# A chunked-attention and gated-MLP kernel: its first steps rebuilt, with signs of weights on GpSimd, loads for two units at a time, all attention products on quarters of the array, and a written order for every engine

## The chip, the cores and the metric

One core of a Trainium2 chip. The metric is the device time of one launch in microseconds (us), median of a few runs. A profiled execution gives the trace that is read here; its own time stands beside its span below.

## The reference

Attention within chunks of 64 tokens, then a gated MLP on the result (4608 tokens, model width 512, hidden width 1536):

```
scores = scale * np.matmul(q_c, k_c.transpose(0, 1, 2, 4, 3))   # 8 batches, 8 heads, 9 chunks of 64, D = 64
scores = scores - np.max(scores, axis=-1, keepdims=True)
attn = np.exp(scores)
attn = attn / (np.sum(attn, axis=-1, keepdims=True) + 1e-09)
out = np.matmul(attn, v_c)
...
gate = 1.0 / (1.0 + np.exp(-(x @ w_gate)))
val = x @ w_val
return (gate * val @ w_out).astype(np.float32)
```

## The kernel before

**Number formats.** Weights arrive as 64-bit floats, as pairs of 32-bit words. The kernel makes of each a high part in fp32r and a low part (value minus high part), and does the same with activations; a product is then three matmuls: high by high, high by low, low by high.

**Tiling.** The tokens are cut into 9 blocks of 512. A block has four *units* (half of its tokens, half of the heads: `units`, L142). For a unit the kernel makes the scores (`products`, L171), a softmax (`scores` L236, `softmax` L257), transposes of the weights of attention (`transposes`, L270), and the values (`values`, L283), which write the block's activations `xt` as high and low part. Units 0 to 7 make the blocks 0 and 1. In these, two heads share one product: the keys of a unit lie in `kbd`, a tile whose off-diagonal halves were set to zero (L76 to L82), and likewise `pbd` for the transposed weights of attention. From unit 8 on, units go in pairs through `products2` (L186) and `values2` (L205), in which each product uses a 64 x 64 quarter of the array and nothing is zero-filled.

**The MLP.** The hidden width is cut into 12 pieces f. `up` (L312) is 12 matmuls over the tokens of a step (G for the gate, V for the value); `hidden` (L326) makes both and the product behind them: sigmoid on ACT (L329), product on DVE (L331), high part on ACT (L334), low part on DVE (L335). `down` (L340) adds the step to the output, three matmuls per 128 tokens. For block 0 the pieces f = 0 and 1 go in two *half steps* of 256 tokens each (`a`, `b`), and all later f in steps of 512 tokens. Blocks 0 to 2 are done in this way; blocks 3 to 8 go in pairs by another scheme (from L505 on), which the change leaves alone.

**Weights.** A piece f has three parts: gate (0), value (1), out (2), each a load of 128 x 1024 words (512 KB, `load_weights` L101). `convert_weights` (L112) turns a part into high and low: two scalings on ACT (L131, L132), a shift on DVE (L133), the sign bit put in (L134), an addition (L136), the high part on ACT (L138) and the low part on DVE (L139). Raw words lie in the tiles of later pieces (slots of f = 9 to 11), so a load must wait until the part that was there is converted.

**What sets the order.** `START` (L29) and `MIDDLE` (L35) are lists of steps: L loads q and k of a unit, V its v, S or s makes the scores (s with the exponentials on ACT and their sums), E, t/T and A the rest; W loads weights, C converts a part, H0.3 is f = 3 of block 0, D a down product. Inside START no engine's order is written: the tool that builds the program orders the instructions of all engines by its own costs, with the list as priority. From MIDDLE on, TensorE follows the list exactly, and from `rest` on DVE and ACT do too. While START runs, weights of block 0 are also stored again in DRAM for the later blocks (`given`, `stream`, L378).

At the very start eight products of a zero tile into an unused bank (`sink`, L92) are queued on TensorE.

Of the kernel before, what the change touches and what calls it, by code (L numbers as in the profile page):

```python
# [15 lines left out]
P = 128  # L16
# [11 lines left out]

START = """  # L29
L0 L1 V0 W0o S0 s1 V1 E0 W0u t0 C0.0 E1 L2 t1 L3 C0.1 A0 W1u S2 C0.2 s3 A1 C1.0 H0.0a E2 W1o E3 C1.1  # L30
T2 W2u T3 D V3 L4 V2 C2.0 A2 C1.2 A3 L5 H0.1a H0.0b W3o D W3u C2.1 C3.0 H0.1b D s4 W4u W2o H0.2 C3.2
C2.2 W4o C3.1 C4.0 D W5u E4 C4.1 C5.0 C5.1 H0.3 D s5 C4.2 t4 E5 W6u H0.4 D W7u C6.0 V5 W6o C7.0 C6.1
H0.5 D W5o L6 C5.2 L7 C6.2 H0.6 V4 W8u C7.1 D W7o C8.0 t5 C8.1 C7.2 H0.7 D W9u
"""
MIDDLE = """  # L35
C9.0 W8o C8.2 W9o C9.1 W10u A4 A5 H0.8 W10o D C10.0 C9.2 C10.2 W11u H0.9 C10.1 D H0.10 C11.0 C11.1 D
W11o H0.11 S7 V7 S6 D L9 E6 H1.0a C11.2 D V6 E7 T6 T7 D H1.1a A6 A7 D H1.0b L8 V8 H1.1b V9 D
"""

VECTOR_TRANSPOSES = 8  # L40
# [10 lines left out]
def chunk_attn_moe(ctx: ExitStack, tc: tile.TileContext, q, k, v, w, out, outt):  # L51
# [17 lines left out]
    early = xp.tile([P, 4, 8, D], F32, tag="x", name="early")  # L69
    zeros = early[:, 0, 0].bitcast(mybir.dt.bfloat16)  # L70
    nc.vector.memset(zeros, 0.0)

    kp = ctx.enter_context(tc.tile_pool(name="kp", bufs=1))
    kbd = [kp.tile([P, 2, 2, 256], F32, tag=f"k{i}", name=f"kbd{i}") for i in range(2)]
    pbd = [kp.tile([P, 8, 2, D], F32, tag=f"p{i}", name=f"pbd{i}") for i in range(2)]
    for i in range(2):  # L76
        eng = nc.gpsimd if i else nc.vector
        eng.memset(kbd[i][0:D, :, 1, :], 0.0)
        eng.memset(kbd[i][D:P, :, 0, :], 0.0)
    for i in range(2):  # L80
        nc.gpsimd.memset(pbd[i][0:D, :, 1, :], 0.0)
        nc.gpsimd.memset(pbd[i][D:P, :, 0, :], 0.0)  # L82
    make_identity(nc, ident)
# [17 lines left out]
    def load_weights(f, kind):  # L101
        if kind == "o":
            raws[f, 2] = stage("spare" if f == NF - 1 else f"o{NF - 1 if f == NF - 2 else NF - 1 - f % 2}", 1024)
        elif f == NF - 1:
            raws[f, 0], raws[f, 1] = stage(f"o{f}", 1024), stage("spare", 1024)
        else:
            raw = stage(f"u{NF - 1 if f == NF - 2 else NF - 1 - f % 2}", 2048)
            raws[f, 0], raws[f, 1] = raw[:, :1024], raw[:, 1024:]
        for part in (2,) if kind == "o" else (0, 1):
            nc.sync.dma_start(raws[f, part], w[f, :, part * 1024:(part + 1) * 1024])  # L110

    def convert_weights(f, part):  # L112

        words = raws.pop((f, part)).rearrange("p (n two) -> p two n", two=2)
        low, high = words[:, 0, :], words[:, 1, :]
        if part == 0:
            both = wp.tile([P, 2, 1024], F32R, tag=f"u{f}", name="w")
            wt[f, 0], wt[f, 1] = both[:, :, :512], both[:, :, 512:]
        elif part == 2:
            wt[f, 2] = wp.tile([P, 2, 512], F32R, tag=f"o{f}", name="w")  # L120
        hi, lo = wt[f, part][:, 0], wt[f, part][:, 1]
        if f < 9:
            slot = 9 if f == 8 else 9 - f % 2
            if part == 0:
                spare[f] = stage(f"u{slot}", 2048)
            val = stage(f"o{slot}", 1024)[:, :512] if part == 2 else spare[f][:, 512 * part:512 * (part + 1)]
        else:
            val = mp.tile([P, 512], U32, tag="ob", name="w_val")
# [831 lines left out]
```

## Time and profile before

| | |
|---|---|
| median of 3 runs | 913.32 us (912.51 to 915.12) |
| the profiled execution | 913.89 us, span 912.1 us |
| TensorE busy | 885.3 us |
| VectorE (DVE) busy | 622.0 us |
| ScalarE (ACT) busy | 417.1 us |
| GpSimd (POOL) busy | 273.6 us |
| mean granted TensorE clock | 0.989 |

PE is TensorE, PEld its weight loads, which run beside its matmuls. In a row of the timeline stand start, duration, engine, line, operation, tiles (out <- in), shapes, count, and in brackets how long the engine was idle before and what ended it. In a row of groups stand count, busy time, mean ns of one, and idle time with its releasers. In a row of windows stand the stretch, its length, busy time (instructions) of each engine named, the granted clock (1.00 is full), the busy share of the DMA engines and GB/s. A busy TensorE isn't TensorE at its peak: matmuls overlap. fp32 products leave two records each, so that 16 products of scores show as 32.

### The profile page before, as it was taken

What the parts mean: (1) busy time and instruction counts of PE and PEld (TensorE: products, weight loads), DVE (VectorE), ACT (ScalarE), POOL (GpSimd) and SP (SyncE); (2) the same over time, 40 slices, a digit from 0 to 9 for tenths busy, and PEclk for the clock granted to TensorE, in tenths of its full rate; (3) what the DMA queues carried; (4) which work ended last, traced back from release to release, by engine and by line L of the source; (5) the groups of instructions that cost most, each with busy time, mean ns of one, the idle gap of its engine ahead of it and who ended that gap; (6) DMA issues with size and microseconds to landing.
All of it is one profiled execution on the core that took longest, in us unless ns stands there. A gap on an engine that the chain in (4) does not pass through costs nothing. (4 is left out here: it accounts for less than half of the span.)

```text
span 912.1 us, 15127 instructions
## 1 busy us (share of the span) xinstructions
PE 885.3 (97%) x5748; PEld 724.9 (79%) x5748; DVE 622.0 (68%) x906; ACT 417.1 (46%) x738; POOL 273.6 (30%) x343
## 2 busy tenths in 40 slices
PE   6999999999999999999999999999999999999998
PEld 3788779888778787877778888888788888888886
DVE  5899885368758787666657995566579943434884
ACT  5889754345425463344453632455335321112441
POOL 1000000168757892256561000353510002432000
PEclk6899999999999999999999999999999999999999
DMA  8599895145554466578784568765545685454553
GB/s 257 204 286 301 279 333 187 47 140 175 173 182 140 145 200 213 182 247 271 226 309 144 202 221 276 257 242 204 178 139 207 210 295 205 171 206 161 185 208 116
DMA packets 93432, 189.74 MB, mean 208 GB/s; under 512 B 8240, under 2 KB 48688, under 8 KB 89520
## 3 DMA queue, kind: packets, MB, share of 16 engines
q1 hardware_dynamic: 93360, 188.78, 61.5%
q8 instruction: 46, 0.75, 0.3%
q14 instruction: 26, 0.21, 0.1%
HBM read 146.28 MB, written 42.47 MB: 207 GB/s over the span
## 5 line engine op out<-in xcount | busy, mean ns | idle before, releaser
L320 PE MATMUL g<-xt,w 128*128 128x512 f32 (+1 forms) x960 | 209.9, 373 | 7.0 <-ACT hf L329 5.1
L320 PEld LDWEIGHTS g<-xt,w 128*128 128x128 f32 x960 | 168.0, 190 | 43.6 <-ACT hf L329 8.9
L651 PE MATMUL d<-hd,wd 128*128 128x512 f32 x756 | 172.4, 389 | 0.1
L651 PEld LDWEIGHTS d<-hd,wd 128*128 128x128 f32 x756 | 141.7, 188 | 30.3 <-DVE hd L631 0.9
L505 PE MATMUL cy<-xc,wr 128*128 128x512 f32 x648 | 159.4, 389 | 0.6 <-DVE s1u L523 0.6
L505 PEld LDWEIGHTS cy<-xc,wr 128*128 128x128 f32 x648 | 121.5, 188 | 26.2 <-DVE s1u L523 1.0
L505 PE MATMUL cx<-xc,wr 128*128 128x512 f32 x432 | 110.7, 391 | 0.0
L505 PE MATMUL cz<-xc,wr 128*128 128x512 f32 x432 | 109.9, 390 | 0.2
L346 PE MATMUL acc<-w,hx 128*128 128x512 f32 x432 | 106.0, 393 | 0.0
L533 POOL TENSOR_TENSOR hid<-u,hid 128x512 f32<-128x512 f32 x15 | 19.4, 1290 | 269.5 <-DVE u L562 269.5
L505 PEld LDWEIGHTS cz<-xc,wr 128*128 128x128 f32 x432 | 80.9, 188 | 17.8 <-issue 1.0
L505 PEld LDWEIGHTS cx<-xc,wr 128*128 128x128 f32 x432 | 80.5, 188 | 17.0
L346 PEld LDWEIGHTS acc<-w,hx 128*128 128x128 f32 x432 | 80.0, 188 | 16.9 <-ACT xt L308 0.2
L415 POOL TENSOR_TENSOR a_val<-a_val 128x128 f32<-128x128 f32 x36 | 18.7, 520 | 239.1 <-DVE a_val L406 180.6
L521 ACT COPY s1u<-cx 128x512 f32<-128x512 f32 x36 | 21.1, 587 | 112.3 <-PE cx L505 107.9
L630 ACT CAST hd<-hid 128x1024 fp32r<-128x1024 f32 x48 | 49.9, 1051 | 49.2 <-PE d L651 37.3
L631 DVE TENSOR_TENSOR hd<-hid,hd 128x1024 fp32r<-128x1024 f32 x48 | 58.4, 1221 | 12.4 <-ACT hd L630 12.2
L778 ACT COPY pt<-pr 32x256 f32<-32x256 f32 x130 | 52.4, 403 | 26.0 <-DVE pr L766 24.2
L331 DVE TENSOR_TENSOR hf<-g,hf 128x512 f32<-128x512 f32 (+1 forms) x40 | 25.3, 632 | 41.7 <-PE g L320 26.4
L523 DVE TENSOR_TENSOR s1u<-cy,s1u 128x512 f32<-128x512 f32 x36 | 24.7, 686 | 38.2 <-PE cy L505 38.2
L334 ACT CAST hx<-hf 128x512 fp32r<-128x512 f32 (+1 forms) x40 | 23.2, 580 | 60.1 <-DVE hf L331 60.1
L562 DVE TENSOR_TENSOR hid<-cz,u 128x512 f32<-128x512 f32 x18 | 12.4, 692 | 55.3 <-PE cz L505 55.2
(125 smaller groups left out, 1188.4 us busy)
## 6 DMA issues: line engine op xcount, KB each, us to landing
wr<-sums SPq DMA_DIRECT2D x72, 512.0 KB, 4.6
wd<-stream SPq DMA_DIRECT2D x30, 1024.0 KB, 4.8
w_raw<-w_in SPq DMA_DIRECT2D x36, 512.0 KB, 5.1
wr<-given SPq DMA_DIRECT2D x36, 512.0 KB, 3.7
qt<-q_in SPq DMA_DIRECT2D x36, 256.0 KB, 4.0
vt<-v_in SPq DMA_DIRECT2D x36, 256.0 KB, 3.4
given<-w SPq DMA_DIRECT2D x36, 256.0 KB, 4.8
wr<-given SPq DMA_DIRECT2D x36, 256.0 KB, 2.8
```

The lines of the kernel that those rows point to most:

```text
L320: nc.tensor.matmul(ps[:, tok], lhsT=wt[f, which][:, wpart, c:c + P], rhs=x[:, part, i, tok], start=n == 0, stop=n == 11)
L331: nc.vector.tensor_tensor(out=hf, in0=pv, in1=hf, op=ALU.mult)
L334: nc.scalar.copy(hh[:, tok], hf)
L346: nc.tensor.matmul(acc[m, t], lhsT=hx[:, ts], rhs=wt[f, 2][:, wpart], start=f == 0 and i == 0, stop=f == NF - 1 and i == 2,)
L505: nc.tensor.matmul(bank, lhsT=lhs(wpart, c), rhs=x[:, part, c], start=start and k == 0, stop=stop and k == 5, skip_group_check=True)
L521: nc.scalar.copy(s1, x)
L523: nc.vector.tensor_tensor(out=u2, in0=y, in1=s1, op=ALU.add)
L533: eng.tensor_tensor(out=h, in0=value, in1=h, op=ALU.mult)
L630: nc.scalar.copy(t[:, 0], at)
L631: nc.vector.tensor_tensor(out=t[:, 1], in0=at, in1=t[:, 0].bitcast(F32), op=ALU.subtract)
L651: nc.tensor.matmul(bank, lhsT=w[:, o:o + P], rhs=x[:, part], start=p == 0 and opening and i == 0, stop=p == 5 and i == 2, skip_group_check ...
L778: eng(pb[dst, :, c, i, :], ps[src, h::2, k, :])
```

## The change

A new list, `OPENING`, takes the place of the first two fifths of START, and **every engine's order** in it is written: TensorE, DVE, ACT, GpSimd and the queue of loads follow it as it stands. The rest of START comes behind it on DVE and ACT. Its words are single steps: `w.f.part` loads a part; `qk.p` and `vv.p` load q and k, and v, of pair p (units 2p and 2p+1); `a p b d h l` are the steps of a conversion; `scores max sub exp sum inv mul turn ca cd av` are the attention of a pair, where i = 0 and i = 1 are the two heads that share a product's place (i = 0 has one exponential over 128 x 512, i = 1 eight with sums); `xh` and `xl` write the high and low part of an activation; `G g V m hh hl D` are a half step; `fill.n` are n products of no use into the bank `sink`, now read from the identity tile.

```diff
+OPENING = """
+w.0.0 qk.0 w.0.1 vv.0 qk.1 w.0.2 w.1.0 w.1.1 w.1.2 a.0.0 p.0.0 b.0.0 d.0.0 fill.14 scores.0 h.0.0 max.0.1 a.0.1
...
+"""
 START = """
-L0 L1 V0 W0o S0 s1 V1 E0 W0u t0 C0.0 E1 L2 t1 L3 C0.1 A0 W1u S2 C0.2 s3 A1 C1.0 H0.0a E2 W1o E3 C1.1
...
+L4 W3o p4 W4u H0.2 C3.1 C3.2
```

**A conversion.** The shift and the sign step become one DVE instruction; GpSimd makes the sign, by multiplying the high word by 0.0 in place. All 36 conversions change so.

```diff
-        nc.vector.tensor_scalar(out=val, in0=val, scalar1=3, scalar2=None, op0=ALU.logical_shift_left)
-        nc.vector.scalar_tensor_tensor(
-            out=val, in0=high, scalar=0x80000000, in1=val, op0=ALU.bitwise_and, op1=ALU.bitwise_or)
-        nc.vector.tensor_tensor(out=val, in0=val, in1=low, op=ALU.add)
+        if step == "p":
+            nc.gpsimd.tensor_scalar(
+                out=high.bitcast(F32), in0=high.bitcast(F32), scalar1=0.0, scalar2=None, op0=ALU.mult)
+        elif step == "b":
+            nc.vector.scalar_tensor_tensor(
+                out=val, in0=val, scalar=3, in1=high, op0=ALU.logical_shift_left, op1=ALU.bitwise_or)
+        elif step == "d":
+            nc.vector.tensor_tensor(out=val, in0=val, in1=low, op=ALU.add)
```

**Loads.** q, k and v of a pair are one load each of 512 KB (the host lays them out so), in one buffer instead of two. q and k of pair 0, and the first weights, now stand ahead of all else in the queue, in the order w.0.0, q, k, w.0.1, v, q, k, w.0.2, w.1.0, w.1.1, w.1.2; before, it was q and k of units 0 and 1 in six loads, then v and weights in turn.

```diff
-        qt = ap2.tile([P, 2, 256], F32, name="qt")
-        nc.sync.dma_start(qt, q[g, u].rearrange("p (a n) -> p a n", a=2))
-        if j < 8:
-            kb = kbd[j % 2]
-            for i in range(2):
-                s = slice(i * D, (i + 1) * D)
-                nc.sync.dma_start(kb[s, :, i, :], k[g, u, s].rearrange("p (a n) -> p a n", a=2))
...
+        g = j // 2
+        qt = ap2.tile([P, 2, 2, 256], F32, tag="pr" if g == 1 else "qt", name="qt", bufs=1)
+        nc.sync.dma_start(qt, q[g].rearrange("p u (a n) -> p u a n", a=2))
+        keys[g] = kp.tile([P, 2, 2, 256], F32, tag="k1" if g else "k0", name="kt")
+        nc.sync.dma_start(keys[g], k[g].rearrange("p u (a n) -> p u a n", a=2))
```

**Quarters.** `products`, `values`, `kbd` and `pbd` are gone, with their zero fills; units 0 to 7 go in pairs through `products2` and the products of `values2` too. The eight products at the start become `fill`:

```diff
-    for _ in range(8):
-        nc.tensor.matmul(sink, lhsT=zeros, rhs=zeros.unsqueeze(1).broadcast_to([P, 4, P]), start=True, stop=True)
+    def fill(times):
+        for _ in range(times):
+            nc.tensor.matmul(
+                sink, lhsT=blank[:, :P], rhs=blank[:, P:].unsqueeze(1).broadcast_to([P, 4, P]), start=True, stop=True)
...
+    with tc.manual_schedule(engines={mybir.EngineType.PE}):
+        with tc.manual_schedule(engines={
+                mybir.EngineType.DVE, mybir.EngineType.Activation, mybir.EngineType.Pool, mybir.EngineType.SP}):
+            for token in OPENING.split():
+                begin(token)
```

**The order on TensorE**, from the first scores on, before (`sc` scores, `tp` transposes, `av` values, `g_296` and `g_311` the gate and value banks of the first half step, `acc` down products):

```order
L179 MATMUL sc<-kbd_90,qt 64x128 x8
L179 MATMUL sc<-kbd_91,qt 64x128 x8
L274 MATMUL tp<-ident,early 128x128 x8
L290 MATMUL av<-pbd_92,vt 64x128 x8
L179 MATMUL sc<-kbd_90,qt 64x128 x8
L320 MATMUL g_296<-xt,w 128x256
L320 MATMUL g_311<-xt,w 128x256
L179 MATMUL sc<-kbd_91,qt 64x128 x8
L320 MATMUL g_296<-xt,w 128x256 x5
L320 MATMUL g_311<-xt,w 128x256 x3
L290 MATMUL av<-pbd_93,vt 64x128 x8
```

and now, with fills (14, 12, 4 and 6 of them) where lines are left out at first:

```order
L190 MATMUL sc<-kt,qt 64x64 x32
...
L298 MATMUL tp<-ident,early 128x128 x8
L205 MATMUL av<-pt,vt 64x64 x32
...
L394 MATMUL g_360<-xt,w 128x256 x12
L394 MATMUL g_377<-xt,w 128x256 x12
L298 MATMUL tp<-ident,early 128x128 x8
L205 MATMUL av<-pt,vt 64x64 x32
L420 MATMUL acc<-w,hx 128x512 x6
L394 MATMUL g_482<-xt,w 128x256 x12
```

Before, units came one by one and the first half step was cut up between scores and values; now the scores of both pairs stand first, the first half step is whole and lies between the values of pair 0 and the transposes of pair 1, and from the values of pair 1 on TensorE has only half steps and down products until the scores of units 4 and 5, which stand ahead of H0.2.

**The order on DVE**, from the first maximum on, before (`mx` maxima, `early` the softmax, `sums` and `inv` its sums and their reciprocals, `w_raw` and `w` weights):

```order
L240 TENSOR_REDUCE mx<-sc 128x8
L249 TENSOR_TENSOR early<-sc,mx 128x512
L240 TENSOR_REDUCE mx<-sc 128x8
L251 TENSOR_SCALAR mx<-mx 128x8
L262 TENSOR_REDUCE sums<-early 128x8
L265 TENSOR_SCALAR sums<-sums 128x8
L267 RECIPROCAL inv<-sums 128x8
L268 TENSOR_TENSOR early<-early,inv 128x512
```

and now, from its first weight on:

```order
L142 SCALAR_TENSOR_TENSOR w_raw<-w_raw 128x512
L145 ISA w_raw<-w_raw 128x1024
L270 TENSOR_REDUCE mx<-sc 128x8 x2
L275 TENSOR_SCALAR mx<-mx 128x8
L272 TENSOR_TENSOR early<-sc,mx 128x8x64
L149 TENSOR_TENSOR w<-w_raw,w 128x512
L142 SCALAR_TENSOR_TENSOR w_raw<-w_raw 128x512
L145 ISA w_raw<-w_raw 128x1024
L287 TENSOR_SCALAR sums_177<-sums_177 128x8
L289 RECIPROCAL inv<-sums_177 128x8
L285 TENSOR_REDUCE sums_177<-early 128x8
L291 TENSOR_TENSOR early<-early,inv 128x8x64
```

Weights come ahead of the first maximum and between the steps of the softmax (L142 is step b, L145 d, L149 l); before, the first conversion stood behind the softmax of units 0 and 1.

**The order on ACT**, before, around its first sigmoid (`hf` the gate, `xt` activations):

```order
L260 ACTIVATE early<-early 128x512
L138 CAST w<-w_raw 128x512
L308 CAST xt<-av 128x2x256
L254 ACTIVATE early,sums<-sc,mx 128x64 x8
L329 ACT_TABLE_LOAD
L329 ACTIVATE hf<-g_296 128x256
L138 CAST w<-w_raw 128x512
```

and now, from the same exponential on (`pt` the transposed weights of attention, `hx` the hidden step):

```order
L277 ACTIVATE early<-early 128x8x64
L314 CAST xt<-av 128x256 x4
L281 ACTIVATE early,sums_253<-sc,mx 128x64 x8
L133 ACTIVATE w_raw<-w_raw 128x512
L134 ACTIVATE w_raw<-w_raw 128x512
L328 ACT_TABLE_LOAD
L328 ACTIVATE hf<-g_360 128x256
L147 CAST w<-w_raw 128x512
L303 COPY pt<-tp 128x256
L336 CAST hx<-hf 128x256
L303 COPY pt<-tp 128x256
```

The second pair's exponentials, two scalings and the table load now stand ahead of the copies of the transposes that the values of pair 1 read.

More of the change, by code (lines that the diff above doesn't have):

```diff
@@ L67, in chunk_attn_moe @@
     ident = const.tile([P, P], F32, name="ident")
[L69 to L71 removed]
+    early = xp.tile([P, 2, 2, 8, D], F32, tag="x", name="early")
+    make_identity(nc, ident)
+    blank = ident.bitcast(mybir.dt.bfloat16)
     kp = ctx.enter_context(tc.tile_pool(name="kp", bufs=1))
[L74 to L83 removed]
     warm = sm.tile([P, 1], F32, name="warm", bufs=1)
@@ L142, in chunk_attn_moe @@
+    def convert_weights(f, part):
+        for step in "apbdhl":
+            converting(f, part, step)
     units = [(m, h, u) for m in range(NB) for h in range(2) for u in range(2)]
@@ L188, in products2 @@
             sc = [ps_g.tile([P, 512], F32, tag="g1", name="sc", bufs=1), ps_o.tile([P, 512], F32, tag="acc", name="sc")]
+        elif j == 2:
+            sc = [ps_o.tile([P, 512], F32, tag="acc", name="sc") for _ in range(2)]
         else:
@@ new lines, in begin @@
+    def begin(token):
+        word, *at = token.split(".")
+        if word == "fill":
+            fill(int(at[0]))
+        elif word == "qk":
+            load(2 * int(at[0]))
+        elif word == "vv":
+            load_values(2 * int(at[0]))
+        elif word == "w":
+            load_part(int(at[0]), int(at[1]))
+        elif word in tuple("apbdhl"):
+            converting(int(at[0]), int(at[1]), word)
+        elif word in ("G", "V", "g", "m", "hh", "hl", "D"):
+            half(word, int(at[0]), at[1])
+        else:
+            opening(word, *map(int, at))
@@ L833, in run @@
             load_values(int(arg))
-        elif what in "Ss":
-            scores(int(arg), what == "s")
+        elif what in "Pp":
+            scores2(int(arg), (0, 1) if what == "p" else ())
         elif what == "E":
@@ L839, in run @@
             transposes(int(arg), what == "t")
-        elif what == "A":
-            values(int(arg))
+        elif what == "B":
+            values2(int(arg))
         elif what == "W":
@@ L851, in run @@
             finish()
-    for op in START.split():
-        run(op)
     kept = [(p, which, c) for p in range(6) for which in range(2) for c in range(2)]
@@ L924, in chunk_attn_moe @@
     with tc.manual_schedule(engines={mybir.EngineType.PE}):
+        with tc.manual_schedule(engines={
+                mybir.EngineType.DVE, mybir.EngineType.Activation, mybir.EngineType.Pool, mybir.EngineType.SP}):
+            for token in OPENING.split():
+                begin(token)
+        with ExitStack() as behind_opening:
+            for kind in (mybir.EngineType.DVE, mybir.EngineType.Activation):
+                behind_opening.enter_context(tc.issue_after(
+                    next(x for x in reversed(nc.cur_bb.bb.instructions) if x.engine == kind)))
+            for op in START.split():
+                run(op)
         for op in MIDDLE.split():
```

292 lines of the change are left out of this document (175 added, 117 removed).

## The prediction

> **What bounds the kernel now.** I read the page first, then the busy time of each engine in four stretches, cut where the first product over all 512 tokens starts (51.42 us), where the twelve f of the first block are through (140.38), and at 190. Columns: stretch, length, busy us (instructions) of PE, PEld, DVE, ACT and POOL, then the granted TensorE clock, the share of the DMA engines, GB/s.
>
> ```profile
> 0.00:51.42 51.42, 40.16 (x296) 32.04 (x297) 36.36 (x74) 34.51 (x86) 3.82 (x12) 0.80 0.74 235
> 51.42:140.38 88.96, 87.43 (x430) 70.22 (x429) 79.81 (x147) 70.49 (x142) 0.00 (x0) 1.00 0.94 304
> 140.38:190.00 49.62, 49.62 (x408) 42.86 (x407) 22.79 (x43) 15.56 (x25) 7.01 (x10) 1.00 0.33 112
> 190.00:912.10 722.10, 708.06 (x4618) 579.77 (x4616) 483.06 (x645) 296.58 (x486) 262.76 (x321) 1.00 0.59 201
> ```
>
> TensorE bounds everything from 51 us on (87.43 of 88.96, then 49.62 of 49.62). In the first stretch it is idle for 11.3 us and runs at a mean clock of 0.80. The change rebuilds that stretch; whatever TensorE reaches earlier at 51.42 is carried to the end of the 912.1 us, unless a later stage cannot follow. Next, the clock there, in single microseconds (length, PE busy, clock, DMA share, GB/s), and the first two blocks of q.k products:
>
> ```profile
> 1.00:2.00 1.00, 1.00 (x3) 1.00 0.34 45
> 2.00:3.00 1.00, 1.00 (x4) 1.00 0.83 266
> 7.00:8.00 1.00, 0.00 (x0) 0.67 0.99 372
> 8.00:9.00 1.00, 0.39 (x4) 0.50 0.98 387
> 27.00:28.00 1.00, 1.00 (x14) 0.59 0.91 248
> ```
>
> ```profile
> 5.58 1.10 PE L179 MATMUL sc<-kbd,qt 128*64 128x128 f32 x16 [1.26 <-DMA kbd<-k_in]
> 8.62 1.97 PE L179 MATMUL sc<-kbd,qt 128*64 128x128 f32 x16 [1.94 <-DMA kbd<-k_in]
> ```
>
> The clock falls to half at about 7.3 us, in the gap between two short bursts, and comes back only at about 27.8: the same 16 records take 1.10 us before and 1.97 after. The waits of TensorE in the first 50 us say what the bursts wait for:
>
> ```profile
> PE tp L274 <- DVE early L268: 5.2, 3, 2.9
> PE sc L179 <- DMA kbd<-k_in: 3.2, 2, 1.9
> ...
> PE g L320 <- ACT w L138: 0.8, 1, 0.8
> PE g L320 <- ACT xt L308: 0.7, 2, 0.4
> ```
>
> So the opening is a chain through DMA, softmax on DVE and ACT, and weight conversion, with TensorE at half clock meanwhile. The point that I follow is the first product over 512 tokens (H0.2), since TensorE has the same work ahead of it in both kernels: six units of scores, four of transposes and values, four half steps, three down products.
>
> **The change part by part.** Prices of that work at full clock:
>
> ```profile
> 47.16 3.04 PE L320 MATMUL g<-xt,w 128*128 128x256 f32 x24
> 50.03 1.56 PE L346 MATMUL acc<-w,hx 128*128 128x512 f32 x6
> 51.42 0.40 PE L320 MATMUL g<-xt,w 128*128 128x512 f32 x1
> ```
>
> ```profile
> 135.63 1.97 PE L179 MATMUL sc<-kbd,qt 128*64 128x128 f32 x32
> ...
> 146.00 1.03 PE L274 MATMUL tp<-ident,pr 128*128 128x128 f32 x8
> ...
> 151.21 1.97 PE L290 MATMUL av<-pbd,vt 128*64 128x128 f32 x32
> ```
>
> ```profile
> 211.14 1.16 PE L199 MATMUL sc<-kt,qt 64*64 64x64 f32 x64
> ...
> 223.34 1.16 PE L214 MATMUL av<-pt,vt 64*64 64x64 f32 x64
> ```
>
> From start to start a half step (G and V) takes 2.87 us and a down product 1.39. A pair of units costs 1.97 in the old form and 1.16 on quarters, scores and values alike.
>
> *Quarters, after H0.2:* scores of units 6 and 7, values of 4 and 5 and of 6 and 7: three blocks, each 0.81 less on an engine that is never idle there: **-2.4 us**.
>
> *Loads:* the stream runs from about 2.0 us, and at 387 GB/s in the ninth microsecond, when weights are moved. I give every load of 0.524 MB 1.34 us, and 0.4 until its reader starts (an estimate). The new order is w, q, k, w, v, q, k: k of pair 0 is there at 6.4, the second weights at 7.8, k of pair 1 at 11.8. The old transfers moved only 45 and 266 GB/s in the second and third microsecond; if the start is as slow again, all this comes 1.5 later.
>
> *The chain in the new order.* Durations on ACT and DVE (count, busy us, mean ns of one, idle before):
>
> ```profile
> L132 ACT ACTIVATE w_raw<-w_raw 128x512 uint32<-128x512 uint32 x36 | 24.4, 681 | 0.7 <-DMA w_raw<-w_in 0.7
> ...
> L329 ACT ACT_TABLE_LOAD x5 | 6.4, 1283 | 0.7 <-PE g L320 0.6
> ...
> L334 ACT CAST hx<-hf 128x256 fp32r<-128x256 f32 x8 | 3.3, 410 | 7.2 <-DVE hf L331 7.2
> ```
>
> ```profile
> L139 DVE TENSOR_TENSOR w<-w_raw,w 128x512 fp32r<-128x512 f32 x27 | 18.3, 687 | 5.7 <-ACT w L138 5.3
> ```
>
> and eight exponentials with their sums, on ACT in one block:
>
> ```profile
> 11.60:14.20 2.60, 2.47 (x16) 0.50 1.08 322
> ```
>
> Scores of pair 0 run from 6.4 to 7.6. DVE then has nine instructions of 0.69 in its list up to mul.0.0 and five on 8 columns, which I put at 0.2: 6.2 + 1.0, so 14.8. ACT isn't last: a.0.1 from 7.8 to 9.2, exponentials to 11.7, one of 128x512 to 12.4. Transposes 1.03, last copy 0.4, values 1.16: av.0 ends at 17.6. ACT goes on with four high parts (1.6, to 19.3), eight exponentials (21.8), a.1.1 (1.4, 23.2), the table (24.4), then g, h.0.2, two copies and hh (2.3, 26.7). TensorE meanwhile does G and V of 0.a and the transposes, which fit, and av.1 starts at 26.8. From there it has a dense queue: av.1 1.1, three half steps 8.6, three down products 4.2, scores of units 4 and 5 1.1, together 15.0: H0.2 at 41.8. For hand-overs I add 1.5, what the two waits on w and xt above cost the old order: **43.3** against 51.42, **-8.1 us**. If instructions overlap on ACT as back-to-back ones do, and nothing waits, it is 41, or -10.4.
>
> *Fill products:* 36 instead of 8, in front of work that isn't there yet. Over 512 columns I price one at 0.24, twice one of the 24 in a half step (2.87 / 24 = 0.12). The twelve behind the first scores then end at 7.6 + 2.9 = 10.5, before k of pair 1 at 11.8, and the four behind the second before mul.0.0, so the loads and DVE hide them and I count nothing. At half clock that cover is gone: twelve take 5.8, and what follows comes about 2 us later.
>
> *Signs by GpSimd:* the shift and the sign step become one on DVE. The old shift alone, in the middle stretch:
>
> ```profile
> 51.42:140.38 88.96, 10.86 (x27) 1.00 0.94 304
> ```
>
> So 0.40 for each of the 36 conversions leaves DVE, and a GpSimd instruction over 128x512 comes between ACT's first scaling and DVE's or-step. The trace has no such instruction; its nearest rows are a cast there, and a DVE subtract of two SBUF tensors and a DVE product with one operand in PSUM, in the stage in which GpSimd works too (min/median/max ns):
>
> ```profile
> L419 POOL CAST a_high<-a_val x30: 609/616/1604, 180.8 to 345.7; 128x512 fp32r<-128x512 f32 x30
> ```
>
> ```profile
> L335 DVE TENSOR_TENSOR hx<-hf,hx x40: 412/693/1758, 34.4 to 361.4; 128x512 fp32r<-128x512 f32 x32, 128x256 fp32r<-128x256 f32 x8
> ```
>
> ```profile
> L331 DVE TENSOR_TENSOR hf<-g,hf x40: 416/683/692, 32.9 to 360.0; 128x512 f32<-128x512 f32 x32, 128x256 f32<-128x256 f32 x8
> ```
>
> Beside GpSimd the subtract grows from 693 to as much as 1758 ns and the cast from 616 to 1604; the product with a PSUM operand never grows. All three DVE steps of a conversion read two SBUF tensors. So a sign step takes 0.6 to 1.6 us and takes 0 to 1.07 from DVE; I take 0.7 and 0.4, since only part of DVE's list has two SBUF operands. That equals the 0.40 saved, and I count the swap at 0; its bound is the rival below. The Trainium skill (GPSIMD Engine Reference, Key points) says the same against this change: GpSimd shares its SBUF interfaces with VectorE, with contention where a DVE instruction has two SBUF inputs. The rows agree, and by its section 4.1 a one-input operation on GpSimd would run at about line rate, which is the lower end, 0.61.
>
> *Between H0.2 and 140 us* the list of START stays nearly as it was. DMA share 0.94 and DVE at 79.81 of 88.96 leave little: **+1.0 us** for TensorE waiting on a weight (an estimate; the old order idles 1.53 there; bounds -1.5 and +5).
>
> Sum: -8.1 - 2.4 + 1.0 = -9.5. The profiled execution took 913.89, so 904.4; the median of the runs is 0.6 below it: **903.8 us**.
>
> **The rivals.** *The chain is later and the clock falls once more* (906 to 909). By my chain TensorE is idle from about 24.5 to 26.8, longer than the 1.94 ahead of which the clock fell in the old trace. If it falls, the dense work runs at half until the clock returns. In the old trace work was dense from 24 on and the clock was back at 27.8; one to two such spans of 3.4 cost 1.7 to 3.4 us. A slow start of the loads adds 1.5: 905.5 to 908.7. The Trainium skill (TensorE: Matmul & The Clock Gate, Why this matters for your kernels) asks only that no gap exceed about 3 us; by that the clock would stay, and the sum be my forecast. The two quoted gaps, of 1.26 and 1.94, show it falling with less, so I keep the rival. For the forecast: six fills stand before the half step.
>
> *The last weights set the pace* (912). Columns: start, us, instruction.
>
> ```profile
> 128.63 1.46 DVE L139 TENSOR_TENSOR w<-w_val,w 128x512 fp32r<-128x512 f32 x2
> ```
>
> ```profile
> 129.92 3.28 PE L320 MATMUL g<-xt,w 128*128 128x512 f32 x13
> ```
>
> The first half of f = 11 is finished at about 129.3, and TensorE takes it at 129.92. If loads and staging, not TensorE's pace, set that moment, the start gained is lost there, and only two quarter blocks behind it remain: 913.3 - 1.6 = 911.7. Against it: the lists tie these conversions to TensorE's steps, and DMA needs 0.94 x 88.96 = 83.6 us for a stretch that still has 85.0.
>
> *GpSimd makes DVE the bound* (slower, 915). In the middle stretch DVE loses the 10.86 us of the old shift: 79.81 - 10.86 = 68.95 us, plus 26 conversions with x each. TensorE needs 87.43 - 2.4 = 85.0. DVE is the bound from x = 0.62 on, the whole gain of 10.5 is gone at x = 1.03, and at the worst 1.07 of the row above DVE needs 96.8: 913.3 + 1.3 = 914.6, with the longer opening about 915. For it: the rows. Against it: the row's worst case would have to hold on average.
>
> **How the numbers follow.** Forecast 0.60, later chain 0.22, last weights 0.11, DVE bound 0.07. Of the runs of this kernel, 0.3% (2.7 us) is about what can be told from no change: faster means below 910.6. The forecast and the later chain lie there, and a little of the third (0.02): 0.84; same 0.09, slower 0.07. The range starts at -10.4 - 2.4 - 1.5, 899, which I round to 899.5, and ends behind the later chain, at 909.5: 0.82 of the chance.
>
> **What would show it.** In the profile after: H0.2's first product between 41 and 46 us; clock 1.00 from about 5 us on (a row of 0.5 behind 20 us is the second case); blocks of scores and values at 1.16; the sign step at 0.6 to 0.8 us and DVE's or-step and subtract at a median near 0.7 (above 1.3 is the DVE case); TensorE busy for all but 1 to 3 us between H0.2 and H1.0 (over 8 idle is the third). If H0.2 starts after 48, my chain is wrong; if H0.2 is early and the time isn't, the middle took it back.

## The result, and the profile after

The changed kernel takes **924.74 us** (median of 6 runs, 920.97 to 931.93); the kernel before, 914.23 (6 runs, 912.51 to 920.36). The ratio is 1.0121, with a 95% interval of 1.0078 to 1.0164: about 11 us slower. The forecast was 903.8, with a range up to 909.5. The profiled execution took 924.82, span 923.0.

First the timeline of TensorE in the changed kernel (start, duration, engine, line, operation, shapes, count, idle before it and what ended it):

```profile
7.19 1.16 PE L190 MATMUL sc<-kt,qt 64*64 64x64 f32 x64 [0.35 <-DMA kt<-k_in]
...
12.31 1.16 PE L190 MATMUL sc<-kt,qt 64*64 64x64 f32 x64 [1.26 <-DMA kt<-k_in]
...
27.70 1.16 PE L205 MATMUL av<-pt,vt 64*64 64x64 f32 x64 [1.18 <-ACT pt L303]
...
43.42 5.74 PE L394 MATMUL g<-xt,w 128*128 128x512 f32 x24
49.00 1.52 PE L420 MATMUL acc<-w,hx 128*128 128x512 f32 x6
57.13 5.11 PE L394 MATMUL g<-xt,w 128*128 128x512 f32 x14 [6.61 <-ACT hf L403]
...
148.71 1.48 PE L394 MATMUL g<-xt,w 128*128 128x256 f32 x11
```

The opening does what it was forecast to do: H0.2 starts at 43.42 (43.3 forecast, 51.42 before), a pair's scores or values take 1.16. Then comes a hole of 6.61 us, and H1.0 starts at 148.71 instead of 140.38. In windows (opening; H0.2 to H1.0; the rest), with length, busy time of TensorE, weight loads, DVE, ACT and GpSimd, clock, DMA share and GB/s:

```profile
0.00:43.42 43.42, 35.58 (x487) 25.95 (x487) 34.72 (x69) 31.54 (x86) 17.11 (x16) 1.00 0.92 335
43.42:148.71 105.29, 89.60 (x497) 70.57 (x491) 78.92 (x120) 67.78 (x143) 43.18 (x26) 0.95 0.75 241
148.71:923.00 774.29, 760.00 (x5057) 624.86 (x5055) 504.53 (x690) 315.00 (x516) 271.41 (x331) 1.00 0.57 193
```

The middle stretch takes 105.29 us where it took 88.96; TensorE idles 15.7 us in it, against 1.5, and the clock falls (0.95 in the mean, with 0.5 between 55 and 60 us and between 122.5 and 125). The last stretch takes 774.29 us; before, it took 771.72 (49.62 and 722.10). Yet no engine is full: DVE, the fullest, is busy 78.92 of 105.29. The waits of TensorE and of DVE in that stretch (us in total, times, longest):

```profile
PE g L394 <- ACT hf L403: 11.6, 4, 6.6
PE g L394 <- DVE hf L405: 4.1, 4, 1.5
```

```profile
DVE w_val L142 <- POOL w_raw L139: 8.9, 4, 4.7
```

TensorE waits for sigmoids (L403) and for the product behind them (L405), and DVE waits 8.9 us for the sign step of GpSimd. `w_val` is the staging tile of the last nine conversions, f = 9 to 11. What did ACT do ahead of the sigmoid that ended the 6.61 us?

```profile
49.03 1.28 ACT L246 ACT_TABLE_LOAD   x1
50.33 0.31 ACT L246 ACTIVATE pr<-sc,mx 128x64 f32<-128x64 f32 x1
...
54.68 0.40 ACT L246 ACTIVATE pr<-sc,mx 128x64 f32<-128x64 f32 x1
54.87 0.29 ACT L246 ACTIVATION_READ_ACCUMULATOR pr<-sc,mx 128x1 f32 x1
55.18 1.28 ACT L403 ACT_TABLE_LOAD   x1
56.48 0.60 ACT L403 ACTIVATE hf<-g 128x512 f32<-128x512 f32 x1
```

`p4` in the list of START is one block: a table load, 16 exponentials (units 4 and 5), and the table back, 7.4 us in which ACT does nothing else. The sigmoid of f = 2 stands behind it. Before, unit 4 had eight exponentials there, 3.8 us from one table load to the next, and unit 5 came later; TensorE's next product waited 0.54 us:

```profile
53.19 1.28 ACT L254 ACT_TABLE_LOAD   x1
56.99 1.28 ACT L329 ACT_TABLE_LOAD   x1
58.93 5.76 PE L320 MATMUL g<-xt,w 128*128 128x512 f32 x24 [0.54 <-ACT hf L329]
```

The second mechanism is the late sign. One place where it is seen, over all engines:

```profile
115.33 1.54 POOL L139 TENSOR_SCALAR w_raw<-w_raw 128x512 f32<-128x512 f32 x1 [3.45 <-ACT w_val L133]
...
116.91 0.69 DVE L142 SCALAR_TENSOR_TENSOR w_val<-w_val,w_raw 128x512 uint32<-128x512 uint32 x1 [1.79 <-POOL w_raw L139]
...
118.12 0.75 DVE L229 TENSOR_TENSOR xt<-av,xt 128x256 fp32r<-128x256 f32 x2
118.57 0.70 ACT L228 CAST xt<-av 128x256 fp32r<-128x256 f32 x2 [2.19 <-DVE xt L229]
...
120.02 0.59 ACT L403 ACTIVATE hf<-g 128x512 f32<-128x512 f32 x1
...
120.66 0.50 PE L394 MATMUL g<-xt,w 128*128 128x512 f32 x1 [2.74 <-ACT hf L403]
```

Read it downward: DVE's or-step waits 1.79 for GpSimd. The subtraction of block 1's values stands behind it in DVE's queue; ACT's next high part waits 2.19 for that one's place; the sigmoid stands behind it in ACT's queue; TensorE waits 2.74 for the sigmoid. One late sign has gone through two queues that work in order. Over the whole program the sign step (min/median/max ns, first and last start) is:

```profile
L139 POOL TENSOR_SCALAR w_raw<-w_raw x36: 1538/1577/1914, 5.3 to 132.9; 128x512 f32<-128x512 f32 x36
```

It takes 1.58 us, not 0.7.

### The profile page after: what moved, and what is told of

Read it like the earlier page. It is cut to its first block, busy times and chain, and to the rows that moved or that the text cites. A ratio compares the mean times of both kernels' runs of the same rounds, so it can differ in the third digit from the quotient of the medians.

```text
span 923.0 us, 15658 instructions
## 1 busy us (share of the span) xinstructions
PE 885.2 (96%) x6032; PEld 721.4 (78%) x6032; DVE 618.2 (67%) x877; ACT 414.3 (45%) x744; POOL 331.7 (36%) x373
## 5 line engine op out<-in xcount | busy, mean ns | idle before, releaser
L394 PE MATMUL g<-xt,w 128*128 128x512 f32 (+1 forms) x960 | 210.9, 375 | 17.4 <-ACT hf L403 12.9
L139 POOL TENSOR_SCALAR w_raw<-w_raw 128x512 f32<-128x512 f32 x36 | 59.6, 1670 | 73.6 <-ACT w_raw L133 43.8
L405 DVE TENSOR_TENSOR hf<-g,hf 128x512 f32<-128x512 f32 (+1 forms) x36 | 23.6, 656 | 48.0 <-PE g L394 30.6
```

What stands on the lines that cost most here:

```text
L139: nc.gpsimd.tensor_scalar(out=high.bitcast(F32), in0=high.bitcast(F32), scalar1=0.0, scalar2=None, op0=ALU.mult)
L394: nc.tensor.matmul(ps[:, tok], lhsT=wt[f, which][:, wpart, c:c + P], rhs=x[:, part, i, tok], start=n == 0, stop=n == 11)
L405: nc.vector.tensor_tensor(out=hf, in0=pv, in1=hf, op=ALU.mult)
```

## Experiments

Theories: **1**, the block of exponentials of units 4 and 5 on ACT; **2**, the latency of the sign steps, ahead of a DVE that works in order; **3**, contention, DVE's steps growing beside GpSimd; **4**, the rest of the list is badly ordered otherwise; **5**, falls of the clock later take what is gained. The kernel before ran beside each group on the same chip; its median there stands with the group. These medians lie between 912.40 and 914.44, and each ratio has an interval of some 2 to 3 us to either side, so a difference of 2 us between runs of two groups isn't clear of noise.

One more thing limits what a run can show. Behind the opening the tool makes the order of START's steps on DVE and ACT by its own costs. An edit that changes the number or the kind of these steps (units 4 and 5, or where signs are made) comes with another order too. Two sets of runs keep one order each, but for the steps added. One set is the run with the later signs on DVE, the run with 52 idle steps beside it, and the run with idle steps made from finished weights. The other is the run with all signs on GpSimd and the lists changed, and the run with signs ahead for f below 9.

### First group (before: 912.40)

Units 4 and 5 by subtraction on DVE and one exponential each:

```diff
-L4 W3o p4 W4u H0.2 C3.1 C3.2
+L4 W3o P4 W4u H0.2 C3.1 C3.2
```

> The changed kernel with one letter changed: units 4 and 5 make their softmax with a subtraction on DVE and one exponential per unit on ACT, instead of 16 exponentials with sums in one block on ACT. The changed kernel took 924.74. If that block ahead of the sigmoid of f = 2 is the cause (theory 1), the idle 6.61 us of TensorE at 57.13 goes, with the half clock behind it (worth 2 to 3 us more): H1.0's first product at 139 to 141 instead of 148.71, and about 916. If the latency of the sign steps on GpSimd is the cause (theory 2), 922 to 924. If only DVE is too full because GpSimd slows it (theory 3), it gets worse, since DVE gets two subtractions and two sums more (about 2.7 us): 926.

Measured: 917.32 (ratio 1.0046, 1.0028 to 1.0064), 7.4 below the changed kernel. The hole at 57 is gone; one of 2.41 comes a step later, at 62.47. Theory 1 holds a part: H1.0 comes at 143.03, and the other holes stay (2.88 us at 110.67, for one).

Conversions behind the opening on DVE again (shift, then sign and or):

```diff
     def convert_weights(f, part):
-        for step in "apbdhl":
+        for step in "asdhl":
...
+        elif step == "s":
+            nc.vector.tensor_scalar(out=val, in0=val, scalar1=3, scalar2=None, op0=ALU.logical_shift_left)
+            nc.vector.scalar_tensor_tensor(
+                out=val, in0=high, scalar=0x80000000, in1=val, op0=ALU.bitwise_and, op1=ALU.bitwise_or)
```

> The changed kernel with the 26 conversions behind the opening in the old form (shift and sign on DVE, nothing on GpSimd); the opening keeps its written order and its ten sign steps on GpSimd. Theory 1 (the block of 16 exponentials): the hole at 57 stays, 921 to 924. Theory 2 (latency of the sign steps, 1.6 us each, ahead of a DVE that works in order): the holes behind 60 us (some 9 us) go, and the one at 57 is shorter since the maxima of units 4 and 5 start earlier: 911 to 915. Theory 3 (contention): like theory 2, and the mean of DVE's steps goes back to 0.69 us from 0.72 to 0.83.

Measured: 915.03 (1.0021, 0.9997 to 1.0045), 9.7 below the changed kernel. The waits behind 60 us are nearly gone and the hole at 57 stays as it was (timeline of TensorE in this run):

```profile
57.00 8.62 PE L398 MATMUL g<-xt,w 128*128 128x512 f32 x24 [6.63 <-ACT hf L407]
```

So the sign steps cost about as much as the block or more (the intervals overlap), and not by lengthening it. Both edits together:

> Both of the two edits before together. If theories 1 and 2 each hold a part, H1.0's first product comes at 131 to 134 us and the time is 905 to 908, below both kernels. If the rest of the list behind the opening is badly ordered for another reason (theory 4), it stays above 912.

Measured: 913.48 (1.0010, 0.9992 to 1.0028). The forecast of 905 to 908 failed: the two gains, 7.4 and 9.7, don't add up, and of 17 only 11 come. A new wait of TensorE shows where one part went, so theory 4 holds a part too:

```profile
142.85 0.63 PE L382 MATMUL tp<-ident,pr 128*128 128x128 f32 x4 [2.78 <-DVE pr L376]
```

Unit 7's exponential now stands behind the sigmoid of H1.0, with a table load for each change. Then the sign step alone, put into the kernel before:

```diff
-        nc.vector.tensor_scalar(out=val, in0=val, scalar1=3, scalar2=None, op0=ALU.logical_shift_left)
-        nc.vector.scalar_tensor_tensor(
-            out=val, in0=high, scalar=0x80000000, in1=val, op0=ALU.bitwise_and, op1=ALU.bitwise_or)
+        nc.gpsimd.tensor_scalar(
+            out=high.bitcast(F32), in0=high.bitcast(F32), scalar1=0.0, scalar2=None, op0=ALU.mult)
+        nc.vector.scalar_tensor_tensor(
+            out=val, in0=val, scalar=3, in1=high, op0=ALU.logical_shift_left, op1=ALU.bitwise_or)
```

> The kernel before with nothing but the signs of the weights made by GpSimd, in all 36 conversions. It took 914.2. Theory 2: the longer chain of a conversion costs here too, 5 to 9 us: 919 to 923. Theory 1 (block of exponentials alone): 913 to 916. The prediction's price of nothing for the swap: 914.

Measured: 928.74 (1.0174, 1.0152 to 1.0196), 16 us slower than before and 6 more than theory 2 had. The swap that the prediction counted at nothing costs most where it stands alone. DVE waits 16.0 us for GpSimd up to 160 us; but START's order, made by the tool, is another one here too, so not all of the 16 us is shown to be the step itself.

### Second group (before: 914.38)

Both edits, and unit 7's softmax beside unit 6's:

```diff
-W11o H0.11 P6 V6 D L8 E6 H1.0a C11.2 D E7 T6 T7 D H1.1a B6 D H1.0b V8 H1.1b D
+W11o H0.11 P6 V6 D L8 E6 E7 H1.0a C11.2 D T6 T7 D H1.1a B6 D H1.0b V8 H1.1b D
```

> Both edits (units 4 and 5 subtract on DVE, later conversions on DVE), and E7 moved up beside E6, ahead of H1.0. In the run with both edits unit 7's table load and exponential came on ACT behind the sigmoid of H1.0 and TensorE waited 2.78 us at 142.85. If that order is the cause, the wait goes, H1.2 starts at 154.6 instead of 157.40, and the time is 909 to 912, against 912.4 of the kernel before. If a fall of the clock or a wait later takes whatever is gained (theory 5: the loss behind 345 us isn't chance), it stays at 913 to 914.

Measured: **909.50** (0.9951, 0.9926 to 0.9975): below both kernels, so theory 5 doesn't hold here. This is the best version of the study. The wait of 2.78 is gone, and the middle stretch takes 90.45 us:

```profile
43.28:133.73 90.45, 86.47 (x498) 68.53 (x491) 79.63 (x146) 63.40 (x113) 0.00 (x0) 1.00 0.85 273
```

Contention by itself: conversions behind the opening on DVE, and beside them, on a tile that nobody reads, two steps of the sign's form for each (`signs` is every second word of that tile):

```diff
+            for _ in range(2):
+                nc.gpsimd.tensor_scalar(out=signs, in0=signs, scalar1=0.0, scalar2=None, op0=ALU.mult)
```

> The conversions behind the opening on DVE (as in the run with that edit alone, 915.03), and beside them GpSimd works on a tile that nobody reads: 52 instructions of the sign step's form, two for each conversion, in a row behind the opening. No engine waits for them. Theory 3 (contention between GpSimd and DVE): DVE's subtract and addition grow above 1.0 us on average and the time goes to 920 or more. Theory 2 (only the latency of the step in the chain counts): DVE's steps stay below 0.85 us on average, time 914 to 917. At the end three of these instructions, three on a dense half of the tile and three copies run alone on GpSimd: if the stride of two words makes the step slow, the dense form takes about 0.6 to 0.8 us, else 1.5.

Measured: 930.04 (1.0171, 1.0145 to 1.0197), 15 above the run without them. No engine waits for GpSimd here, so contention is real: its work on SBUF makes DVE's steps longer. They grow less than the 1.0 us that was expected, the addition from 683 to 867 ns. DVE's groups from 43 us on (count, busy us, mean ns), the shift without this work and with it, and with it the product that reads PSUM:

```profile
L145 DVE TENSOR_SCALAR w_raw<-w_raw 128x512 uint32<-128x512 uint32 x17 | 7.0, 419 | 0.0
```

```profile
L151 DVE TENSOR_SCALAR w_raw<-w_raw 128x512 uint32<-128x512 uint32 x17 | 12.7, 749 | 0.0
L415 DVE TENSOR_TENSOR hf<-g,hf 128x512 f32<-128x512 f32 x10 | 6.8, 682 | 2.0 <-PE g L404 1.8 <-ACT hf L413 0.2
```

The shift, with one operand, grows most, from 419 to 749 ns. The product doesn't grow (686 without this work).

The kernel before once more, for a second profile:

> The kernel before, unchanged, for a second profile of it. If the falls of the clock behind 100 us are chance (one to two 3.4 us spells at half clock in each execution, at other places), this one may have one or two and 566.8 us become 568 to 570 from the sixteenth pair of steps to the end; if they belong to the changed kernel, it has none.

Measured: 914.13 (0.9993, 0.9968 to 1.0018). It has a fall of the clock at 412 us, so such falls are no mark of the changed kernel. And H0.2 comes earlier than in the profile that the prediction read:

```profile
47.65 5.60 PE L320 MATMUL g<-xt,w 128*128 128x512 f32 x24
```

Both edits, and the ten sign steps of the opening on DVE too:

```diff
         if step == "p":
-            nc.gpsimd.tensor_scalar(
-                out=high.bitcast(F32), in0=high.bitcast(F32), scalar1=0.0, scalar2=None, op0=ALU.mult)
+            return
         elif step == "b":
-            nc.vector.scalar_tensor_tensor(
-                out=val, in0=val, scalar=3, in1=high, op0=ALU.logical_shift_left, op1=ALU.bitwise_or)
+            nc.vector.tensor_scalar(out=val, in0=val, scalar1=3, scalar2=None, op0=ALU.logical_shift_left)
+            nc.vector.scalar_tensor_tensor(
+                out=val, in0=high, scalar=0x80000000, in1=val, op0=ALU.bitwise_and, op1=ALU.bitwise_or)
```

> Both edits, and the ten conversions of the opening on DVE too: no sign step on GpSimd at all, the written order otherwise as it is. By the chain of the prediction the swap counts nothing for H0.2 (43.4); by theory 2 the ten steps of 1.6 us stand partly on the opening's path, so H0.2 comes earlier, at 41 to 43; if GpSimd relieves DVE there, later, at 44 to 46. Time like both edits, 911 to 915.

Measured: 918.82 (1.0056, 1.0032 to 1.0080), with H0.2 at 48.87, later than any theory said. But the run did more than its edit: a scaling of a later conversion now stands on ACT in front of a copy of the opening's transposes, and waits there for its load (timeline of ACT):

```profile
21.06 0.65 ACT L134 ACTIVATE w_raw<-w_raw 128x512 uint32<-128x512 uint32 x1 [4.38 <-DMA w_raw<-w_in]
21.61 0.35 ACT L303 COPY pt<-tp 128x256 f32<-128x256 f32 x1
```

TensorE waits 4.97 us for what follows. Inconclusive: what the opening's ten sign steps are worth stays open.

### Third group (before: 913.30)

One idle step for each conversion, made from the low words:

```diff
+            nc.gpsimd.tensor_scalar(
+                out=signs, in0=low.bitcast(F32), scalar1=0.0, scalar2=None, op0=ALU.mult)
```

> As the run with sign steps that nobody reads (930.04 with 52 of them in a row, DVE's steps of a conversion up from 0.68 to 0.78 to 0.87 us and its shift from 0.42 to 0.75), but one for each conversion, 26, made from the low words right behind ACT's second scaling, so at the times at which the changed kernel makes its signs. GpSimd's load is that of the changed kernel, and no engine but a later load waits for it. Without any it was 915.03, with signs that DVE waits for 924.74. Contention (theory 3) alone: 921 to 925. Latency (theory 2) alone: 915 to 917. A value between shares the 9.7 us.

Measured: 923.06 (1.0103, 1.0066 to 1.0139). Inconclusive: later loads waited for the idle steps, since these read the raw words (waits of the load queue):

```profile
SPq L108 <- POOL other L148: 8.4, 4, 4.3
```

The changed kernel again:

> The changed kernel, unchanged, beside the others on one chip: 922 to 927, H0.2 within 1 us of 43.42 and again a hole of 6 to 7 us behind the gate of f = 2.

Measured: 923.24 (1.0116, 1.0075 to 1.0157), H0.2 at 43.33, the hole again 6.61. Next the edits to units 4 and 5 and to E7, with all signs on GpSimd (the lists of the run with 909.50, the conversions of the changed kernel):

> The changed kernel with units 4 and 5 subtracting on DVE and E7 beside E6, signs on GpSimd everywhere: the best version (909.5) but for the conversions behind the opening. Theories 2 and 3 both: 5 to 9 us slower than the best version, 914 to 918. If the sign steps only hurt through the hole at 57, 910 to 912.

Measured: 916.69 (1.0042, 1.0016 to 1.0068): 7.2 above the 909.50 of the best version (5.9 above its second run, on this chip, below). TensorE starts f = 8 at 99.38 against 98.18 there, f = 10 at 123.94 against 116.09: most is lost between the two. Signs made ahead for f below 9, with DVE and ACT in the same order:

```diff
     def convert_weights(f, part):
+        if f < 9:
+            sign(f, part)
...
+    def sign(f, part):
+        high = raws[f, part].rearrange("p (n two) -> p two n", two=2)[:, 1, :]
...
+        nc.gpsimd.tensor_scalar(
+            out=signs[f, part].bitcast(F32), in0=high.bitcast(F32), scalar1=0.0, scalar2=None, op0=ALU.mult)
```

> The run before with GpSimd's signs of f below 9 made straight from the loaded words into a free place, not behind ACT's scaling: the order on DVE and ACT is the same, GpSimd's load too, but the step stands beside ACT's and not between ACT and DVE. Latency (theory 2): 3 to 8 us faster than the run before, 909 to 912. Contention (theory 3): the same, within 2 us.

Measured: 915.59 (1.0028, 1.0006 to 1.0051), hardly faster. That looked like contention, but DVE's waits from 95 us on, first in the run before and then in this one, say otherwise:

```profile
DVE w_val L142 <- POOL w_raw L139: 11.7, 6, 4.3
DVE w_val L158 <- POOL w_raw L155: 10.3, 6, 3.2
```

But for one of 1.4 us, all its waits for GpSimd behind the opening lie in the last nine conversions, which this edit had left alone.

### Fourth group (before: 913.27)

A clean form of the idle step: it reads the high part just made, which no load overwrites:

```diff
         elif step == "h":
             nc.scalar.copy(hi, val.bitcast(F32))
...
+            nc.gpsimd.tensor_scalar(out=signs, in0=hi.bitcast(F32), scalar1=0.0, scalar2=None, op0=ALU.mult)
```

> The conversions behind the opening on DVE, and for each of the 26 one step of the sign's form on GpSimd that reads the high part just made (nobody overwrites it before the middle blocks) and writes a tile that nobody reads: no load and no engine waits for it. Orders of DVE, ACT, TensorE and loads are those of the run without it (915.03). Contention (theory 3): 920 to 925. Latency (theory 2): 914 to 917.

Measured: 919.70 (1.0076, 1.0050 to 1.0102), 4.7 above the run without (915.03), between the two expectations. The orders on DVE and ACT are the same, so this is contention at the changed kernel's load, with the old shift still on DVE. All signs ahead (the lists of the run with 916.69), those of f = 9 to 11 into a tile that is free there:

```diff
-        if f < 9:
-            sign(f, part)
+        sign(f, part)
```

> As the run with signs ahead (915.59), and the signs of f = 9 to 11 ahead too, into a tile that is free there. GpSimd's load stays; DVE's waits of 10.3 us for GpSimd should go. Latency (theory 2): 909 to 912. Contention (theory 3): 914 to 917, with DVE's idle time ended by other releasers.

Measured: 911.58 (0.9987, 0.9969 to 1.0005), 5.1 below the run with no sign made ahead (916.69). DVE's wait there falls from 11.7 to 3.9 us:

```profile
DVE w_val L163 <- POOL w_sign L128: 3.9, 2, 2.4
```

GpSimd's 26 steps and their contention are all still there (DVE's addition at 751 to 784 ns). DVE and ACT keep their order but for some neighbours exchanged in the last nine. And the other way round, the best version with GpSimd's signs in f = 3 to 8 and DVE's in the last nine:

```diff
-        for step in "asdhl":
+        for step in "apbdhl" if f < 9 else "asdhl":
```

> The best version with the 17 conversions of f = 3 to 8 behind the opening on GpSimd again; f = 9 to 11 stay on DVE. If the cost sits in the last nine (where the run with all signs on GpSimd lost 6.7 us between f = 8 and f = 10): 909 to 911, like the best version. If it is spread evenly: 913 to 915.

Measured: 910.86 (0.9980, 0.9957 to 1.0003). The best version again:

> Units 4 and 5 subtracting on DVE, E7 beside E6, all conversions behind the opening on DVE, unchanged, beside the others on one chip: 907 to 911, 3 to 6 us below the kernel before.

Measured: 910.81 (0.9971, 0.9951 to 0.9991). By the medians the two are equal, and putting the last nine on DVE is worth 5.8 us (916.69 with all 26). That the other seventeen cost nothing isn't shown: the intervals leave room for 2 to 3 us, and in the profiles H1.0 comes 3.3 us later with them on GpSimd (137.06) than here. A second thing shows in the profile of this run:

```profile
45.75 5.74 PE L398 MATMUL g<-xt,w 128*128 128x512 f32 x24
133.81 3.04 PE L398 MATMUL g<-xt,w 128*128 128x256 f32 x24
```

H0.2 starts 2.5 us later than in the first profile of this version (43.28), because the clock fell to 0.5 from 27.5 to 32.5 us, and H1.0 starts at the same time (133.73 there). What is gained at H0.2 isn't all carried on.

### Last group (before: 914.44)

The kernel before, for a third profile:

> The kernel before, unchanged, for a third profile: H0.2's first product between 47 and 52 us, later with a longer stretch at half clock in the opening. The changed kernels of this study stood at 43.1 to 43.5 each time but one.

Measured: 911.55 in one run. The first product over 512 tokens again stands 4 us earlier than in the profile that was read, and H1.0 comes 6 us earlier (134.34 for 140.38; 135.44 in the second profile):

```profile
47.42 5.64 PE L320 MATMUL g<-xt,w 128*128 128x512 f32 x24
134.34 3.04 PE L320 MATMUL g<-xt,w 128*128 128x256 f32 x24
```

The last sentence of the expectation doesn't hold. Of the fourteen profiles by then with the opening of the changed kernel, eleven have H0.2 at 43.05 to 43.64, but three at 44.16, 44.81 and 45.75; with the opening's signs on DVE it was 48.87.

The best version with the block put back:

```diff
-L4 W3o P4 W4u H0.2 C3.1 C3.2
+L4 W3o p4 W4u H0.2 C3.1 C3.2
```

> The best version (910.8, 909.5) with the block of 16 exponentials on ACT for units 4 and 5 put back. Theory 1, the block costs by itself: the hole of 6.6 us behind the gate of f = 2 is back, with a fall of the clock, and the time is 914 to 917. If what the hole takes is made up behind it because ACT or DVE or the loads set the pace there: 910 to 912.

Measured: 912.96 (0.9977, 0.9952 to 1.0002). The hole is back (5.79 us at 57.14). The median is 2.2 to 3.5 us above the two of the best version, between the two expectations, but by the ratios the difference is 0.5 to 2.4 us, within the intervals. In the profile, of a slow execution (916.91), H1.0 comes at 140.16, 6.4 us late, so there the hole isn't made up. What the block costs by itself stays open.

## Why the prediction was wrong

**Right.** The chain of the opening: H0.2 at 43.42 for 43.3, and blocks of 1.16. Its single dates came a little late (scores of pair 0 at 7.19 for 6.4, values of pair 1 at 27.70 for 26.8), and the 1.5 us for hand-overs covered that. The clock stayed at 1.00 through the opening, and the rival with a later chain didn't come; but that was in part luck. In four of the fifteen profiles with this opening the clock did fall, near 27.5 us, behind waits of 1.0 to 1.2 us that the others have too, and H0.2 came at 44.16 to 45.75. (One sum of the chain is off: 14.8 and 1.03, 0.4 and 1.16 make 17.4, not 17.6, so that its own terms give 43.1.) The test that the prediction named came out as written: H0.2 was early and the time wasn't, so the middle took it back.

**The step that failed** is the one for the middle: "Between H0.2 and 140 us the list of START stays nearly as it was", with +1.0 us and bounds of -1.5 and +5. With two quarter blocks in it the stretch should have taken 88.3 us (88.96, less 1.6, plus 1.0); it took 105.29, so the term came out at about +18. Of these, 14.2 are more idle time of TensorE, and 3.8 longer products at the lower clock (89.60 busy for 85.8). Three things were wrong in the term, and two in what the sum was built on.

*The list had changed.* `s4` before H0.2 and `s5` behind H0.3 had become one `p4`. By the run that undoes it this costs 7.4 us in the changed kernel; once the signs are out of the way, the cost isn't clear of noise in the medians. The prediction had no term for it. The 16 exponentials in ACT's queue ahead of a sigmoid could be read from the change.

*The sign step takes 1.58 us, not 0.7.* The nearest row was the wrong one: a cast of 512 columns. The top of the bounds, 1.6, is what came. By its occupancy that would have cost DVE nothing, because the contention was about as priced: DVE's three steps of a conversion (groups of the changed kernel from 43 us on, but for the last nine: count, busy us, mean ns) are

```profile
L142 DVE SCALAR_TENSOR_TENSOR w_raw<-w_raw 128x512 uint32<-128x512 uint32 x18 | 15.6, 877 | 2.3 <-POOL w_raw L139 2.3
L145 DVE CUSTOM_DVE_ANT_0 w_raw<-w_raw 128x1024 uint16<-128x1024 uint16 x18 | 14.2, 804 | 0.1
L149 DVE TENSOR_TENSOR w<-w_raw,w 128x512 fp32r<-128x512 f32 x19 | 13.8, 732 | 2.0 <-ACT w L147 2.0
```

Against 0.68 to 0.69 each with GpSimd idle, that is 0.36 more for a conversion (0.4 was forecast), and the shift saved is 0.42. So the rival in which GpSimd makes DVE the bound didn't come: it needed 0.62, and DVE is busy 78.92 of 105.29.

*The swap was priced by occupancy and not by latency.* A sign step lies in the chain of its conversion, and the last nine conversions have two staging tiles among them (`ob`), so none can run far ahead: DVE stands still for 8.9 us and holds up ACT and TensorE. Four runs on one chip show this: signs of all f on GpSimd 916.69; ahead for f below 9, 915.59; ahead for all, 911.58; last nine on DVE, 910.86. So about 6 us of the loss are the sign steps (916.69 against 910.81), 5 of them waits in these nine. The rival "the last weights set the pace", whose sign was TensorE idle for more than 8 us, had named the right place, with a price of giving back the gain and not of going beyond it.

*The baseline was one execution.* In the profile that was read, the opening was slow (51.42) and the rest free of clock falls. Two more profiles of the same kernel have H0.2 at 47.65 and 47.42. Against these the opening gains 4 us, not 8.1.

*What is gained at H0.2 isn't all carried to H1.0.* The prediction carried it to the end, unless a later stage cannot follow. In the two profiles of the best version one cannot: H1.0 starts at 133.73 and 133.81, whether H0.2 starts at 43.28 or 45.75. Before H1.0, TensorE waits 1.0 and 0.4 us for weights and 2.3 for products in H0.4 and behind it. Against the 135.44 and 134.34 of the kernel before, the lead at H1.0 is about 1 us and not 4. What sets the pace there was not tested.

From 924.7 to 903.8, then: 924.7 to 916.7 by the lists (units 4 and 5, E7), and to 910.2 by the signs (the mean of 909.50 and 910.81). Of the last 6.4, 2 lie ahead of H1.0, which the best version reaches at 133.73 and 133.81 and the forecast at 131.6 (43.3 and 88.3). The other 4 lie behind H1.0, in a stretch whose length differs between executions, in part by falls of the clock. In the profile that was read it took 771.72 us, with no fall; in the other two of the kernel before 775.16 and 775.36, with one and two falls. The best version has 770.87 with one fall (the execution of 906.43 us) and 778.19 with three. So the profile that was read paired a slow opening with a fast rest, and the sum counted on speeding up the one and keeping the other. This last account is read from five profiles, not tested.

What stays open: what the block costs without the late signs, and what sets the pace between H0.2 and H1.0 in the best version.

## What to carry to other kernels

Price an instruction that moves to another engine twice: by the time it takes from each engine, and by what waits for its result, in the queues behind the waiting one. Where only two staging tiles feed a chain, a microsecond in the chain counts (nine conversions, 5.8 us); where conversions can run ahead, the same step is much cheaper (seventeen, nothing in the medians, some 3 us in the profiles). And read the baseline from more than one profile before a gain of one per cent is worked out from one of them.

## What the runs showed of the hardware

GpSimd's multiplication by a scalar doesn't get cheaper on dense data. The run with 52 idle steps had nine more instructions on GpSimd, at 480 to 496 us (min/median/max ns, first and last start): a multiplication on every second word, one on dense data, and a dense copy:

```profile
L1026 POOL TENSOR_SCALAR one<-one x3: 1537/1562/2419, 479.8 to 491.5; 128x512 f32<-128x512 f32 x3
```

```profile
L1027 POOL TENSOR_SCALAR one<-one x3: 1483/1492/1492, 483.6 to 493.2; 128x512 f32<-128x512 f32 x3
```

```profile
L1028 POOL COPY one<-one x3: 612/1482/1484, 485.2 to 494.7; 128x512 f32<-128x512 f32 x3
```

The stride is worth 0.07 us. The copy takes 0.61 in one case, and 1.48 in the two that run beside DVE instructions on SBUF tiles. The Trainium skill (GPSIMD Engine Reference, Key points) says that GpSimd contends with a DVE instruction in a two-port performance mode or with two SBUF inputs. The addition's 683 to 867 ns, with two SBUF inputs, and the unchanged 682 of the product that reads PSUM agree; the shift's 419 to 749, with one input, would agree if it runs in such a mode, which no run here shows.

The clock falls later in the program too, after small gaps, for one spell at a time. The run with both edits, in windows of 2.5 us (length, busy TensorE, clock, DMA share, GB/s):

```profile
600.00:602.50 2.50, 0.42 (x12) 0.94 0.87 313
602.50:605.00 2.50, 2.50 (x10) 0.50 0.45 120
605.00:607.50 2.50, 2.50 (x11) 0.87 0.77 308
```

The clock's shortfall there adds up to 3.4 us at half speed, which costs 1.7 us of full-speed work. In the twenty profiles every spell costs 1.7 us or a multiple of it, but for two of less than 0.3 us at the very end. The spell shown follows a gap of 2.21 us in the middle of a block of scores, in which TensorE waited for nothing that the profile shows; nine of the twenty profiles have such a gap, of 0.7 to 2.3 us, and the others none. Other spells follow waits of 2.04 us (295 us, all signs ahead) and of 0.99 us (381 us, the run with 909.50); but the first profile of the kernel before has waits of up to 1.0 us at such places too, and no spell behind 100 us. So the length of the gap alone doesn't decide it. Profiles of the kernels here have between none and three such spells behind 100 us, those of the kernel before too. Of the 24 runs of the best version, those at the two ends show what that is worth: mean clock 0.990, 910.5 to 914.5 us (4 runs); 0.998 and above, 906.4 to 909.1 (6 runs).
